# Linear attention with a top-2 mixture of experts on one core: early rows for four experts, the order of loads on two DMA queues, and longer gaps between row scatters

## The chip, the core and the metric

The kernel runs on one core of a Trainium2 chip. The core has a matrix engine (PE, with a separate record for its weight loads, PEld), a vector engine (DVE), a scalar engine (ACT), GpSimd (POOL) and a sync engine (SP). POOL and SP issue most of the transfers; all transfers of the core share 16 DMA engines. The metric is the device time in microseconds (us) of one execution. A run's time differs from execution to execution, so the median of several is compared. The profile comes from one execution; its span runs from the first to the last instruction.

## What is computed

```python
def _attn_ref(q, k, v):                       # q, k, v: 8 batches x 8 heads x 576 x 64
    q_p, k_p = phi(q), phi(k)                 # phi(x) = x + 1 if x > 0 else exp(x)
    kv = einsum('bhsd,bhse->bhde', k_p, v)
    z = sum(k_p, axis=2)
    num = einsum('bhsd,bhde->bhse', q_p, kv)
    den = einsum('bhsd,bhd->bhs', q_p, z)[..., None] + 1e-06
    return num / den

def _moe_ref(x, w_gate, w_noise, noise, w1, w2):    # x: 4608 tokens x 512
    noisy_logits = x @ w_gate + log1p(exp(x @ w_noise)) * noise     # 4608 x 8
    top2 = the two largest of each row; top2_w = their softmax
    for e in range(8):
        for k in range(2):
            mask = top2[:, k] == e
            h = maximum(x[mask] @ w1[e], 0.0)       # 512 -> 1024
            out[mask] += top2_w[mask, k, None] * (h @ w2[e])        # 1024 -> 512
```

Each token is thus worked on by two of eight experts. All matrix work is in bf16 with sums in float32.

## The kernel before

**Attention.** The tokens are taken in four groups of two batches (1152 tokens, nine columns of 128 each). For each group POOL issues the loads of k, q and v, in halves (L158, with a cast from float32 to bf16 on the way). ACT computes the exponential, DVE the rest of phi, PE the products; `num` (L262 to L295) makes x and the router's inputs: PE multiplies (L272), DVE divides (`rden` L279, `xr` L283, `lwt` L290).

**Routing.** `UNITS` cuts the tokens into five units: one for each of the first three groups, and two of six and three columns for the last. For each unit `rt_a`, `rt_b` and `rt_c` (L298 to L385) find the two experts of every token, its two gates and, with prefix sums on PE, its place `posi` in each expert's list. Each expert has two lists: "F" holds tokens for which it is the expert visited first (of lower number), "S" those which it visits second. `dispatch(u, a, z)` (L391) then writes the rows of x into these lists in device memory (`x_sorted`): for every column of 128 tokens and each of its two slots one indirect transfer issued by POOL (L398), followed by `apart()` (L387), a memset of a scratch tile `gap` on POOL that does nothing but take time. There are 72 such scatters.

**Early rows.** A list is complete only when all five units are dispatched. `ROUNDS` and `EARLY` (L34, L35) set bounds: after unit 0, 1 and 2, the places of the first `EARLY` experts' lists below a bound are known to be filled, because later ranks of those lists start at the bound at least (L380 to L384: the running count `carry` is raised to it). Blocks of early rows may be loaded before the later units are dispatched. Before the change the early blocks are of experts 0, 1 and 2: two blocks of expert 0 of two tiles each (a tile is 128 rows; the second of these is called `a1` in `attention` and `a0` in `routing`), then `a1` = (1, F, tiles 0 to 2), `b0` = (0, F, 4 and 5), `b1` = (1, F, 3 and 4), `a2` = (2, F, 0 to 3): 15 tiles, 1920 rows. The first block from complete lists is `c0` = (0, F, from tile 6).

**The experts.** `PLAN` lists the further blocks of every expert, of tiles of three kinds: F (first visits, result stored into `part`, L661 on SP), S (second visits: the first expert's result is gathered from `part` by L613 on POOL, added, and the sum scattered to the output by L667 on POOL), and M, a mixed tile with the ends of both lists, whose rows are gathered by `mid_gather` into `xm` (L499 to L509, POOL). `interval(cur, prev, weights, nxt)` (L677) writes down the order: `mm1` of the current block (L630 on PE, relu on ACT L632) alternates with `mm2` and `put` of the block before (L645 on PE; gate on DVE L649 to L653; store), and with the transposes of the next (L592 on PE, copy on ACT L596); then come the gathers of the next block and one or two halves of a later expert's weights (`w_load`, L438, issued by POOL at L442; 1 MB each as it lands). The table `todo` (L989 to L993) says with which block which half goes. Loads of rows (`xn_load`, L556 to L569) and of their gates (`meta_load`, L444 to L455) are issued by SP.

**What sets the order.** Attention and experts are written down in one fixed order per engine; nothing is rearranged. Each engine, and each issuing queue (POOL, SP), works through its instructions in that order, and an instruction that waits holds up all behind it. `general()` at the end is a fallback for lists that don't fit; it does no work on these inputs.

**Places that matter here.** The zero stores (in `attention`, L771 to L778) write `zrow`, a tile of zeros, over the rows that lie behind some lists' ends and are read as padding. Before, they stand on SP ahead of everything but a few loads. The weights of expert 0 are issued by POOL among the last columns of unit 0, those of expert 1 among `dispatch(1)`, those of expert 2 among `dispatch(3)`, those of expert 3 with the first two blocks of the main loop, and those of expert e+2 with the first two blocks of expert e.

Of the kernel before, what the change touches and what calls it, by code (L numbers as in the profile page):

```python
# [9 lines left out]
INT32 = mybir.dt.int32  # L10
# [23 lines left out]
ROUNDS = [(0, (256, 0, 0)), (1, (512, 384, 0)), (2, (768, 640, 512))]  # L34
EARLY = 3  # L35
# [14 lines left out]
def build_constants(tc, consts, w_gate, w_noise, noise):  # L50
# [23 lines left out]
    c["gap2"] = tile_("gap2", [P, 352])  # L74
    c["gap"] = c["gap2"][:, 0:192]
# [336 lines left out]
class PhaseB:  # L412


    def __init__(self, ctx, tc, w1, w2, x_sorted, part, out):
        self.tc, self.nc = tc, tc.nc
        self.w1, self.w2, self.x_sorted, self.part, self.out = w1, w2, x_sorted, part, out
        pool = lambda name, bufs: ctx.enter_context(tc.tile_pool(name=name, bufs=bufs, side="left"))
        self.wp = [pool("B_w", 2)]
        self.mp, self.xp, self.hp = pool("B_m", 2), pool("B_x", 3), pool("B_h", 2)  # L420
        self.yp = [pool("B_y", 3)]
        self.lp = self.np = None
        self.ps_h = self.ps_y = self.ps_t = None
        self.count = {}
        self.w, self.m, self.x = {}, {}, {}

        self.left, self.ready = [0] * 6 + [1] * 5 + [2] * 4, set()
# [329 lines left out]

def attention(pa, pb, c, x_sorted, zrow):
# [12 lines left out]
    nc.vector.memset(zrow[:], 0.0)  # L771

    for e, kind, i, n in ((0, "F", 8, 2 * P), (3, "F", 4, P), (4, "S", 4, P), (7, "S", 8, 2 * P), (E, "S", 0, 1)):
        row = pb.row(e, kind, i)
        for a in range(0, n, P):
            nc.sync.dma_start(out=x_sorted[row + a : row + min(n, a + P), :], in_=zrow[0 : min(P, n - a)])
    nc.sync.dma_start(out=pb.part[NO_P : NO_P + 1].bitcast(INT32)[:, 0 : ROW_W // 2], in_=zrow[0:1])
    nc.sync.dma_start(out=pb.part[NO_P : NO_P + 1].bitcast(INT32)[:, HD - ROW_W // 2 : HD], in_=zrow[0:1])  # L778
# [25 lines left out]
    for g in range(3):  # L804
# [4 lines left out]
        pa.phi(n, "k")  # L809
        if g < 2:  # L810
            pa.load(g + 2, "q")
# [71 lines left out]
def routing(pa, pb, c, first):  # L883
# [11 lines left out]
    pb.meta_load(2, "F", 0, 4, 2)  # L895
    pb.xn_load(a2, 2)
# [6 lines left out]
    pa.dispatch(3, 0, 3)  # L903
    pb.w_load(2, 0)
    pa.dispatch(3, 3, 6)
    pb.w_load(2, 1)
# [32 lines left out]
def kernel(  # L939
# [24 lines left out]
    with ExitStack() as order:  # L964
# [24 lines left out]
        todo = {0: (3, 0), 1: (3, 1)}  # L989
        for e in range(2, E - 2):  # L990
            at = [i for i, b in enumerate(blocks) if b["e"] == e][:2]
            for k, i in enumerate(at):
                todo[i] = (e + 2, k)  # L993
        for i, b in enumerate(blocks):
            pb.left += [b["e"]] * sum(kind != "S" for kind, _ in b["tiles"])
        for i, b in enumerate(blocks):
# [10 lines left out]
            if i in todo:  # L1007
                e2, k = todo[i]
                if k == 0 and e2 > 3:
                    pb.w_tiles(e2, {4: 1, 5: 2}.get(e2, 0))  # L1010
# [35 lines left out]
```

## Time and profile before

| | us |
|---|---|
| median of 7 runs | 462.21 |
| lowest, highest | 457.38, 466.95 |
| the profiled execution | 467.89 |
| its span | 466.0 |

| engine | busy us in the span | share |
|---|---|---|
| PE | 366.1 | 79% |
| PEld | 218.1 | 47% |
| DVE | 185.2 | 40% |
| ACT | 194.4 | 42% |
| POOL | 275.3 | 59% |

The mean granted clock of PE in that execution is 0.890 of full speed. The transfers move 85.59 MB at a mean of 184 GB/s.

How to read it: the shares are means over stages that differ. Attention lies in the first 160 us or so, with PE about half busy at most; the dispatches run on POOL from about 65 to 196; the experts' products fill PE behind that. Three views are used below. The windows give, for a stretch of time, the busy time of each engine with its number of instructions, the granted clock of PE and the mean busy share of the DMA engines (which can exceed one, since packets overlap). The chain of what ended last goes back from the last instruction: at every step to what released it. The timeline lists one engine's instructions with the idle time before each and what ended it. In them `x_sorted<-xr,posi` is a scatter of dispatch, `xn<-x_sorted` a load of rows, `xm<-x_sorted,m_idx` the gather of a mixed tile and `w<-in_moe_w_dram` a load of weights.

### The profile page before, as it was taken

The page shows a single profiled execution, that of the slowest core. Times are in us where ns is not written, and L with a number is a line of the kernel's source. Part 1 is how long each engine was busy: PE and PEld are TensorE (multiplying, and loading weights), DVE is VectorE, ACT ScalarE, POOL GpSimd, SP SyncE. Part 2 cuts the span into 40 slices and gives each one's busy share as a digit, 9 for nine tenths or more (in the row PEclk, how much of TensorE's full clock was granted, in tenths as well). Part 3 has the DMA queues.
Part 4 walks back from the last instruction along what each step waited for, and adds up shares of the span by engine and source line. Part 5 has one row for each costly group of instructions (what it writes and reads, how often), then busy time and mean ns, then how long its engine had stood idle before and what let it go on. Part 6 is the DMA issues. An engine that isn't in the chain of part 4 may idle for free.

```text
span 466.0 us, 7157 instructions
## 1 busy us (share of the span) xinstructions
PE 366.1 (79%) x2641; PEld 218.1 (47%) x2641; DVE 185.2 (40%) x471; ACT 194.4 (42%) x321; POOL 275.3 (59%) x408
## 2 busy tenths in 40 slices
PE   3594465663633688998999999799999899999990
PEld 1383454552511445543565545445555445554450
DVE  2737989895433564111233222041331131231231
ACT  1718562651520254543354553245345235445410
POOL 7120238988888158650036636349648865877781
PEclk9757767567975699999999999989999989999996
DMA  9999994797953339966349597985995996745531
GB/s 129 209 231 207 208 207 141 156 225 170 214 190 109 115 94 253 245 183 171 113 141 247 181 212 214 244 211 174 259 213 163 216 229 184 247 148 160 160 139 36
DMA packets 63010, 85.59 MB, mean 184 GB/s; under 512 B 15887, under 2 KB 45714, under 8 KB 62966
## 3 DMA queue, kind: packets, MB, share of 16 engines
q0 software_dynamic: 36160, 63.91, 61.9%
q1 hardware_dynamic: 25142, 20.96, 15.1%
q10 hardware_dynamic: 1664, 0.18, 0.5%
q8 instruction: 22, 0.36, 0.3%
q14 instruction: 22, 0.18, 0.1%
HBM read 83.88 MB, written 33.79 MB: 252 GB/s over the span
## 4 chain that ended last, share of the span: by engine, by line
PE 48%; DMA 23%; DVE 9%; POOL 8%; another core or an unknown queue 4%; issue 4%; ACT 2%; POOLq 0%; DVEq 0%; ACTq 0%; SPq 0%
PE b L630 23%; PE b L645 22%; DMA kq<-in_q_dram 5%; DMA xm<-x_sorted,m_idx 5%; POOL x_sorted L398 4%; DMA xn<-x_sorted 3%; PE t L592 3%; DMA w<-in_moe_w_dram 3%; DMA x_sorted<-xr,posi 3%; DMA kq<-in_k_dram 2%; DMA part<-y 1%; ACT e L178 1%; DVE xr L283 1%; POOL L L613 1%
## 5 line engine op out<-in xcount | busy, mean ns | idle before, releaser
L630 PE MATMUL b<-xt,w 128*128 128x256 bf16 (+5 forms) x832 | 152.7, 331 | 9.1 <-ACT xt L596 4.1
L645 PE MATMUL b<-w,hT 128*128 128x512 bf16 (+1 forms) x640 | 146.3, 384 | 0.0
L632 ACT ACTIVATE hT<-b 128x256 bf16<-128x256 f32 (+5 forms) x208 | 98.9, 484 | 104.1 <-PE b L630 95.3
L630 PEld LDWEIGHTS <-w 128*128 128x128 bf16 x832 | 81.2, 101 | 65.5 <-issue 13.1
L398 POOL DMA_INDIRECT x_sorted<-xr,posi x72 | 74.8, 1039 | 36.0 <-issue 25.2
L645 PEld LDWEIGHTS <-hT 128*128 128x128 bf16 (+1 forms) x640 | 59.6, 100 | 66.0 <-issue 5.6
L596 ACT COPY xt<-t 128x1024 bf16<-128x1024 bf16 x30 | 30.4, 1012 | 52.6 <-PE t L592 48.6
L613 POOL DMA_INDIRECT L<-part,mgi x12 | 12.0, 1001 | 56.8 <-DMA xn<-x_sorted 35.7
L178 ACT ACTIVATE e<-kq 128x2304 bf16<-128x2304 bf16 x16 | 33.3, 2123 | 25.3 <-DMA kq<-in_k_dram 9.5
L667 POOL DMA_INDIRECT out_dram<-y,si x34 | 33.8, 993 | 13.6 <-DVE y L649 8.8
L613 POOL DMA_INDIRECT L<-part,gi x34 | 34.8, 1023 | 6.9 <-issue 5.4
L272 PE MATMUL num<-kvbd,pqt 128*64 128x162 bf16 x288 | 17.6, 287 | 22.9 <-DVE lwt L290 20.6
L209 PEld LDWEIGHTS <-e 64*128 64x128 bf16 x288 | 21.8, 125 | 18.3 <-DVE e L190 13.8
L209 PE MATMUL b<-v,e 64*128 64x192 bf16 x144 | 20.4, 318 | 9.6 <-DVE e L190 6.5
L272 PEld LDWEIGHTS <-pqt 128*64 128x64 bf16 x288 | 14.4, 139 | 25.7 <-issue 14.6
L209 PE MATMUL misc<-v,e 64*128 64x192 bf16 x144 | 20.3, 318 | 5.8 <-DMA v<-in_v_dram 5.8
L592 PE MATMUL t<-ident,xn 128*128 128x128 bf16 (+1 forms) x256 | 20.5, 218 | 4.5 <-DMA xn<-x_sorted 3.4
L667 POOL DMA_INDIRECT out_dram<-y,msi x12 | 11.8, 979 | 20.8 <-DVE y L649 9.1
L592 PEld LDWEIGHTS <-xn 128*128 128x128 bf16 (+1 forms) x256 | 17.0, 98 | 13.1 <-DMA xn<-x_sorted 4.4
L651 DVE TENSOR_SCALAR y<-b,meta2F 128x512 f32<-128x512 f32 x14 | 10.4, 750 | 31.5 <-PE b L645 17.9
L283 DVE TENSOR_TENSOR xr<-num,rden 128x768 bf16<-128x768 f32 x24 | 21.9, 953 | 2.5 <-DMA x_sorted<-xr,posi 2.1
L389 POOL MEMSET gap<- 128x192 f32 x72 | 22.1, 306 | 0.0
(170 smaller groups left out, 362.8 us busy)
## 6 DMA issues: line engine op xcount, KB each, us to landing
w<-in_moe_w_dram POOLq DMA_DIRECT2D x16, 1024.0 KB
part<-y SPq DMA_DIRECT2D x39, 256.0 KB
kq<-in_k_dram POOLq DMA_DIRECT2D x8, 576.0 KB
kq<-in_q_dram POOLq DMA_DIRECT2D x8, 576.0 KB
v<-in_v_dram POOLq DMA_DIRECT2D x8, 576.0 KB
xn<-x_sorted SPq DMA_DIRECT2D x11, 256.0 KB
xn<-x_sorted SPq DMA_DIRECT2D x6, 384.0 KB
xn<-x_sorted SPq DMA_DIRECT2D x4, 512.0 KB
```

Of the source, the lines that this page charges most:

```text
L178: self.nc.scalar.activation(out=e, in_=x, func=ACT.Exp)
L209: nc.tensor.matmul(out=self.kvps[g, h, j][:, KVM * i : KVM * i + KVM], lhsT=e[half, hp, ci, :], rhs=v[half, hp::4, 64 * ci : 64 * ci + 64] ...
L272: nc.tensor.matmul(out=ps[half, hp, KVW * i : KVW * i + KVW], lhsT=self.pqt[g, 3 * t + i][:, hp, half], rhs=self.kvbd[g][:, j, hp, :], sta ...
L283: nc.vector.tensor_tensor(out=_ap(xr, [[64, 4], [ROW_W, 3], [1, 64]], off=3 * t * ROW_W + 256 * s), in0=_ap(ps, [[512, 4], [KVW, 3], [1, 6 ...
L398: r = self.nc.gpsimd.indirect_dma_start(out=self.x_sorted, out_offset=bass.IndirectOffsetOnAxis(ap=self.r["posi", u][:, ci - c0, sl : sl + ...
L592: nc.tensor.transpose(ps[:, i, dc, 0:m], self.xn(b, t, dc), self.c["ident"][0:m, 0:m])
L596: nc.scalar.copy(out=b["xt"][:, :, t * P : t * P + 2 * P].rearrange("p c (i r) -> p i c r", i=2), in_=ps)
L613: r = nc.gpsimd.indirect_dma_start(out=L[0:m].bitcast(INT32), out_offset=None, in_=self.part.bitcast(INT32), in_offset=bass.IndirectOffset ...
L630: nc.tensor.matmul(out=ps[:, 0:n], lhsT=w1[:, dc, fc * P : fc * P + P], rhs=b["xt"][:, dc, 0:n], start=(dc == 0), stop=(dc == 3))
L632: nc.scalar.activation(out=b["hT"][:, fc, 0:n], in_=ps[:, 0:n], func=ACT.Relu)
L645: nc.tensor.matmul(out=ps[i * m : i * m + m], lhsT=b["hT"][:, f, t * P : t * P + m], rhs=w2[:, f, :], start=(fc == 0), stop=(fc == 8 // n ...
L667: r = nc.gpsimd.indirect_dma_start(out=self.out, out_offset=bass.IndirectOffsetOnAxis(ap=self.m[e, kind, i]["si"][0:m], axis=0), in_=y[0:m ...
```

## The change

It has seven parts.

1. Early rows for a fourth expert: the bounds get a fourth column. The block of four tiles of expert 2 becomes two of two tiles (`a2`, `b2`), and a block `a3` of the first three tiles of expert 3 comes early: 18 tiles, 2304 rows in all. `a2` lies below the bounds of unit 1 and is taken right behind `a1`. Expert 3's plan loses the same three tiles.
2. The memset between dispatch scatters covers 288 elements for each partition, not 192; that after gathers and output scatters 416, not 352.
3. The zero stores move behind the first group's `phi(1, "k")` and stand in a function of their own.
4. Weights move on POOL's queue: expert 1's from `dispatch(1)` into the first columns of `dispatch(2)`; expert 2's from `dispatch(3)` into the last columns of `dispatch(2)`; expert 3's from the main loop into `dispatch(4)`. The weights of experts 4 to 7 are loaded one expert earlier, with the first two blocks of expert e-3.
5. The early rows' gates get tiles of their own, and the loads of all early blocks stand on SP ahead of the stores of the blocks they overlap: `a1` and `a2`, then `b0` and `b1` ahead of the first stores in `routing`, `b2` and `a3` ahead of those of the intervals.
6. The load of `c0` follows the fourth of the five early intervals.
7. The last early interval has no next block; the transposes of `c0` follow it.

```diff
-ROUNDS = [(0, (256, 0, 0)), (1, (512, 384, 0)), (2, (768, 640, 512))]
-EARLY = 3
+ROUNDS = [(0, (256, 0, 0, 0)), (1, (512, 384, 256, 0)), (2, (768, 640, 512, 384))]
+EARLY = 4
...
-    c["gap2"] = tile_("gap2", [P, 352])
-    c["gap"] = c["gap2"][:, 0:192]
+    c["gap2"] = tile_("gap2", [P, 416])
+    c["gap"] = c["gap2"][:, 0:288]
...
-        m = self.mp.tile([P, nt, 4], INT32, name=f"meta{nt}{kind}")
+        m = self.mp.tile([P, nt, 4], INT32, name=f"meta{nt}{kind}" if group is None else f"early{e}_{i0}")
...
+def zeros(pb, x_sorted, zrow):
+    nc = pb.nc
+    nc.vector.memset(zrow[:], 0.0)
+
+    for e, kind, i, n in ((0, "F", 8, 2 * P), (3, "F", 4, P), (4, "S", 4, P), (7, "S", 8, 2 * P), (E, "S", 0, 1)):
+        row = pb.row(e, kind, i)
+        for a in range(0, n, P):
+            nc.sync.dma_start(out=x_sorted[row + a : row + min(n, a + P), :], in_=zrow[0 : min(P, n - a)])
...
 def attention(pa, pb, c, x_sorted, zrow):
...
-    nc.vector.memset(zrow[:], 0.0)
-
-    for e, kind, i, n in ((0, "F", 8, 2 * P), (3, "F", 4, P), (4, "S", 4, P), (7, "S", 8, 2 * P), (E, "S", 0, 1)):
...
         pa.phi(n, "k")
+        if g == 0:
+            zeros(pb, x_sorted, zrow)
         if g < 2:
             pa.load(g + 2, "q")
...
         elif g == 1:
-            for i in range(2):
-                pa.dispatch(1, 3 * i, 3 * i + 3)
-                pb.w_load(1, i)
-            pa.dispatch(1, 6, 9)
+            pa.dispatch(1)
             pb.xn_load(a1, 1)
...
         else:
-            pa.dispatch(2)
+            for i in range(2):
+                pb.w_load(1, i)
+                pa.dispatch(2, i, i + 1)
+            pa.dispatch(2, 2, 5)
         pa.num(n, 0, 0)
...
-    a2, c0 = pb.block(2, ("F", 0, 4)), pb.block(0, ("F", 6, 4))
+    a2, b2 = pb.block(2, ("F", 0, 2)), pb.block(2, ("F", 2, 2))
+    a3, c0 = pb.block(3, ("F", 0, 3)), pb.block(0, ("F", 6, 4))
     pb.w_tiles(2, 1)
+    pb.w_load(2, 0)
+    pa.dispatch(2, 5, 7)
+    pb.w_load(2, 1)
+    pa.dispatch(2, 7, 9)
     pb.w_tiles(3, 1)
     pb.xn_load(a1, 1)
+    pb.meta_load(2, "F", 0, 2, 1)
+    pb.xn_load(a2, 1)
...
-    pa.dispatch(3, 0, 3)
-    pb.w_load(2, 0)
-    pa.dispatch(3, 3, 6)
-    pb.w_load(2, 1)
+    pa.dispatch(3)
...
-    pa.dispatch(4)
+    pa.dispatch(4, 0, 1)
+    pb.w_load(3, 0)
+    pa.dispatch(4, 1, 2)
+    pb.w_load(3, 1)
+    pa.dispatch(4, 2, 3)
     pb.mids()
-    pb.xn_t(b0, 0)
-    pb.interval(b0, a1, (), b1)
+    pb.xn_t(a2, 0)
+    pb.meta_load(2, "F", 2, 2, 2)
+    pb.xn_load(b2, 2)
+    pb.meta_load(3, "F", 0, 3, 2)
+    pb.xn_load(a3, 2)
+    pb.interval(a2, a1, (), b0)
+    pb.interval(b0, a2, (), b1)
+    pb.interval(b1, b0, (), b2)
+    pb.interval(b2, b1, (), a3)
     pb.prepare(0)
     pb.xn_load(c0)
-    pb.interval(b1, b0, (), a2)
-    pb.interval(a2, b1, (), c0)
-    return a2, c0
+    pb.interval(a3, b2, (), None)
+    pb.xn_t(c0, 0)
+    pb.xn_t(c0, 1)
+    return a3, c0
...
-    3: [[("F", 0, 4)], [("F", 4, 1), ("M", 0, 1), ("S", 0, 1), ("M", 1, 1)], [("S", 1, 2)]],
+    3: [[("F", 3, 2)], [("M", 0, 1), ("S", 0, 1), ("M", 1, 1)], [("S", 1, 2)]],
...
-        todo = {0: (3, 0), 1: (3, 1)}
-        for e in range(2, E - 2):
-            at = [i for i, b in enumerate(blocks) if b["e"] == e][:2]
+        todo = {}
+        for e in range(4, E):
+            at = [i for i, b in enumerate(blocks) if b["e"] == e - 3][:2]
             for k, i in enumerate(at):
-                todo[i] = (e + 2, k)
+                todo[i] = (e, k)
```

More of the change, by code (lines that the diff above doesn't have):

```diff
@@ L425, in __init__ @@
         self.w, self.m, self.x = {}, {}, {}
-        self.left, self.ready = [0] * 6 + [1] * 5 + [2] * 4, set()
+        self.left, self.ready = [0] * 6 + [1] * 5 + [2] * 4 + [3] * 3, set()
     def rot(self, pools, what):
@@ L755, in general @@
                             in_=b["y", 0][:], in_offset=None, bounds_check=N_TOK - 1, oob_is_err=False)
+def zeros(pb, x_sorted, zrow):
[5 more added lines that the diff above has]
+            nc.sync.dma_start(out=x_sorted[row + a : row + min(n, a + P), :], in_=zrow[0 : min(P, n - a)])
+    nc.sync.dma_start(out=pb.part[NO_P : NO_P + 1].bitcast(INT32)[:, 0 : ROW_W // 2], in_=zrow[0:1])
+    nc.sync.dma_start(out=pb.part[NO_P : NO_P + 1].bitcast(INT32)[:, HD - ROW_W // 2 : HD], in_=zrow[0:1])
 def attention(pa, pb, c, x_sorted, zrow):
@@ L770, in attention @@
     nc.vector.tensor_copy(out=wblk[64:P, :, 16:32], in_=wst[64:P])
-    nc.vector.memset(zrow[:], 0.0)
-    for e, kind, i, n in ((0, "F", 8, 2 * P), (3, "F", 4, P), (4, "S", 4, P), (7, "S", 8, 2 * P), (E, "S", 0, 1)):
[L774 to L778, printed above, removed]
     pa.rest()
@@ L894, in routing @@
     pb.xn_load(b1, 2)
-    pb.meta_load(2, "F", 0, 4, 2)
-    pb.xn_load(a2, 2)
     pb.xn_t(a1, 0)
@@ L1008 @@
                 e2, k = todo[i]
-                if k == 0 and e2 > 3:
+                if k == 0:
                     pb.w_tiles(e2, {4: 1, 5: 2}.get(e2, 0))
```

## The prediction

> **What bounds the kernel now.** I read the busy shares by window first, then the chain that ended last, then the PE and POOL timelines around each break of PE.
>
> The windows (length, then busy time and instructions of PE, PEld, DVE, ACT, POOL, then granted TensorE clock, DMA share, GB/s):
>
> ```profile
> 40.00:60.00 20.00, 9.71 (x147) 8.15 (x148) 18.50 (x36) 12.78 (x11) 4.07 (x6) 0.73 1.21 208
> 80.00:100.00 20.00, 10.30 (x126) 8.93 (x128) 17.61 (x52) 14.42 (x15) 18.06 (x24) 0.67 0.87 175
> 120.00:140.00 20.00, 8.92 (x118) 5.77 (x115) 7.94 (x33) 6.12 (x11) 17.46 (x29) 0.86 0.79 189
> 140.00:160.00 20.00, 7.86 (x53) 4.82 (x54) 9.02 (x24) 2.27 (x5) 12.46 (x20) 0.59 0.27 96
> 200.00:220.00 20.00, 16.59 (x97) 8.18 (x96) 3.27 (x12) 9.23 (x16) 6.55 (x9) 1.00 0.78 205
> 220.00:240.00 20.00, 20.00 (x129) 11.26 (x127) 6.91 (x16) 7.28 (x17) 0.24 (x1) 1.00 0.35 106
> 300.00:320.00 20.00, 18.19 (x99) 9.03 (x100) 5.60 (x12) 9.22 (x16) 10.57 (x15) 0.91 0.80 205
> ```
>
> Three stages. Attention (to about 106 us) is held by loads and by DVE. From 106 to about 158 nothing is full: PE works 8 to 9 of 20 us, DVE too, and POOL scatters rows. From 158 on PE is the bound: 20.00 of 20.00 in most windows, so there only PE's breaks can be won or added. The chain (start, length, what) and PE's timeline (last bracket: idle time before it and what ended it) name them:
>
> ```profile
> 108.36 3.38 DMA xt<-x_sorted
> 133.15 4.40 another core or an unknown queue
> 138.32 6.37 another core or an unknown queue
> 148.90 5.76 another core or an unknown queue
> 187.63 7.98 DMA x_sorted<-xr,posi
> 206.14 11.30 DMA xn<-x_sorted
> 289.06 12.71 DMA xm<-x_sorted,m_idx
> 364.14 9.76 DMA xm<-x_sorted,m_idx
> ```
>
> ```profile
> 195.91 1.89 PE L630 MATMUL b<-xt,w 128*128 128x512 bf16 x8 [0.90 <-DMA x_sorted<-xr,posi]
> 204.13 0.62 PE L592 MATMUL t<-ident,xn 128*128 128x128 bf16 x8 [1.16 <-DMA xn<-x_sorted]
> 217.49 0.62 PE L592 MATMUL t<-ident,xn 128*128 128x128 bf16 x8 [2.25 <-DMA xn<-x_sorted]
> ```
>
> So the wait for the complete lists costs PE 0.90+1.16+2.25 = 4.3 us. The gathered mixed tiles (xm) of experts 4 and 6 cost it 2.83 (298.98 to 301.81) and 2.55 (371.39 to 373.94). Between 127 and 155, 19.6 us of the chain (4%) belong to "another core or an unknown queue": finished PE matmuls whose results DVE and ACT see 3 to 6 us late.
>
> The sum is against the profiled execution: span 466.0, 1.9 outside it, 467.9, which is 5.7 over the median 462.2. I add the difference to the median.
>
> **The change, part by part.**
>
> Longer gaps. 192 elements take 0.275 us, 352 take 0.413 (both in POOL's timeline): 0.86 ns an element, so 288 take 0.358 and 416 take 0.469. The 72 dispatch gaps add 72 x 0.083 = 6.0 us to POOL; the some 100 gaps of the second half add 5.5. The latter are hidden: POOL works 12 of 20 us there and stood 32 us at 208 to 240. The first 12 precede the last q load on POOL, so that load, both weight loads of expert 0 and the first rows slip by 1.0. That chain is on the path: +1.0.
>
> Zero stores. 0.87 MB leave the start and come back at about 45 us. In the start, halves of k (0.59 MB) land every 2.84 us and with the stores between them every 4.1 to 4.4, so the stores cost the loads 2.8 us. But ACT waited 1.6 for q, and DVE only 0.28 (it was busy until 47.9). Gain: 0.3 and the zrow memset's 0.3 on DVE. The Trainium skill, "DMA: Bandwidth & Descriptors", section "Issuing engines are not separate DMA queues", speaks against more: all initiated DMAs share the same 16 engines and interleave. The row of 40 to 60 says the same (DMA share 1.21, full until about 72): moved bytes are paid there, unless DVE covers them (18.50 of 20). Full price 2.8, full gain 2.8; I take -0.4. Section sum: +0.6. The rule bears equally on the row loads put ahead of the stores on SP: they wait less for their turn (before: up to 9 us behind y), but the bytes travel with the same weights. I count nothing for it alone.
>
> Weights of experts 1 to 3 on POOL. An issue takes 0.95 + 0.2, six of them move, none is added. Expert 1's pair leaves dispatch(1), which with longer gaps still ends at about 129 (before 128.5). Then, at 1.49 a scatter: w(1,0) to 130.4, one column, w(1,1) to 134.5, columns to 146.4. Its first use is at 168.67 (the first matmuls on 384 columns); the slowest weight load of the chain took 12.8, so both halves land by 148. w(2,0) now stands in dispatch(2) and needs the space of attention's last tiles, so it waits for the last num matmul on PE. That one ended at 149.6 but was seen at about 154.7, with the front's slip 155.7. Behind it: four columns (12 us), w(2,1), then 12 scatters of dispatch(3), and dispatch(4) with w(3): 170, 188, 200. Before they ended at 153.95, 184.8, 195.9: the 13.45 us that POOL stood idle before 167.40 are used up. Rows of group 2 land at about 175, b0's load takes 3.4, PE wants it at 182.7: covered. w(2,0) is wanted where b0 had its first matmuls, 177.51, and issued 21 us before: covered. w(3) is wanted at 209 and issued by 199: just covered; 5 us later it would be PE's stall.
>
> More early rows. The block of four tiles of expert 2 is cut in two and three tiles of expert 3 come early: 64 matmuls more, but half as wide (8 of 256 columns 0.87 us, 8 of 512 1.73), so PE's time changes by nothing. 16 more relus of 0.48 on ACT lie in a stage where ACT works 9 of 20. The three tiles are 3 x (1.75 + 1.73) = 10.4 us of PE ahead of the first block from a complete list, which PE then wants at 217.7. Its rows: last scatter 200, landing 4 later as before (195.9 to 199.9), up to 5 more behind w(3,1), and a load of 3.7 (quick) to 11.3 (the slow one of the chain): 208 to 220. Taken: all of the 4.3 us goes; ends 0 and -5.5.
>
> Later weights, one expert earlier. Expert 7's pair no longer travels when expert 6's xm is gathered: -2.55, and the clock. Here the row and a rule differ. After each xm stall eight 256-wide matmuls took 1.71 instead of 0.87 and the windows show 0.91: about 1.3 us. The rule ("TensorE: Matmul & The Clock Gate", Part 1: the clock is halved after an idle window of about 3.4 us) would make that 0 for stalls of 2.8 and 2.55. The trace decides: -3.9; by the rule alone it would be -2.55.
>
> Expert 4's xm loses cover: the block before it has no F tile, and the one before that two for four. So two mm2 tiles (3.46) and some mm1 (1.7 to 2.3) leave between issue and use: wanted 16 us after the interval's start instead of 22, landed at 24.7 as before behind a weight load. The stall grows from 2.8 to at most 8.7; two 256 KB stores fewer should hasten it. Ends 0 and +5.9, taken +4.5. Expert 3's xm now goes behind two weight loads instead of one; DVE waits 5 to 7 us longer there, PE has four banks of work: 0, at worst +3.
>
> Own buffers for early metas remove a 9 us wait on SP, off the path. Three wider bounds: under 0.5 us of DVE in idle time.
>
> Sum: +0.6 - 4.3 - 3.9 + 4.5 = -3.1: 459.1 against 462.2.
>
> **The rivals.**
>
> B, front shrinks. The late results between 127 and 155 coincide with 18 scatters 1.41 apart; the last came when that burst ended (153.95). If the burst causes it, spacing of 1.49 and a pause at w(2,0) cut the 19.6 us; everything behind, up to posi(3) at 166, moves. At half: -10, so 449. For it: the coincidence. Against: no record names the cause, and dispatch(1) made the same scatters without such waits.
>
> C, slower: POOL stands before w(2,0) for PE's last num. With the old lateness there are 9 us or less of slack for the complete lists (208 to 220 against 217.7). Expert 1's weights, 2 MB in all, now fall into the same 130 to 150 us as dispatch(2), where the DMA share was only 0.27 in the window from 140. If that makes the last num later by 8 to 12, then columns 5 to 8, dispatch(3), w(3) and c0's rows all slip as much: 8 to 12 less some cover, on top of -3: 467 to 472. It decides once that wait ends after about 163. For it: the queue order and a chain that is already PE, DVE, ACT in turn there. Against: POOL's pause also lightens the DMA.
>
> D: early rows don't move PE, since the wait shifts onto c0 whole and xm takes back the rest: 462.
>
> **How the numbers follow.** A, the sum above, 0.42 (459; own range 454 to 464), B 0.25 (447 to 453), C 0.28 (466 to 473), D 0.05. Runs of this kernel scatter by about 1%, so 1% is what can be told: faster is below 457.6, slower above 466.8. A gives faster 0.17, same 0.24, slower 0.01; B faster 0.25; C slower 0.28; D same 0.05. Range: 447 to 471 leaves out the ends of B and C.
>
> **What would show it.** In the new profile: PE without a break over 1 us between 180 and 220 (early rows), or one on DMA xn at about 217 (C, D). The idle time before w(2,0) on POOL, and when dispatch(3) starts: 170 in A, 162 or less in B, 178 or more in C. The share of "another core or an unknown queue": 4% in A, 2% in B. PE idle on xm at expert 6 gone, at expert 4 from 2.8 to 7 us. Zero stores showing up as a longer wait of DVE or of the first scatters before 72 us would make the front's term wrong; a PE stall on w anywhere would make the weight terms wrong.

## The result and the profile after

| | kernel before | changed kernel |
|---|---|---|
| median, us | 461.26 (63 runs) | 458.08 (26 runs) |
| lowest, highest | 454.67, 467.73 | 454.27, 461.33 |
| span of the profiled execution | 466.0 | 455.7 |

The ratio of the two is 0.9978, with a 95% interval of 0.9955 to 1.0: no change beyond 0.5%. It is nearer to one than the medians, because the comparison leaves out the runs that lie more than 1.5% above the quickest of their kernel, and 28 of the 63 runs of the kernel before do. The forecast was 459.1 and a gain of 3.1; by the ratio the gain is about 1, a third of that.

Four windows of the changed kernel (busy times of PE, PEld, DVE, ACT, POOL, then PE's clock, DMA share, GB/s), the end shares of its chain, and PE's breaks from its timeline:

```profile
120.00:140.00 20.00, 13.65 (x155) 10.11 (x153) 14.56 (x51) 7.98 (x16) 17.73 (x27) 0.83 0.62 142
140.00:160.00 20.00, 14.60 (x90) 8.62 (x89) 9.35 (x40) 5.88 (x13) 16.73 (x26) 0.83 1.15 269
200.00:220.00 20.00, 17.73 (x113) 10.06 (x111) 3.20 (x12) 10.41 (x21) 5.92 (x8) 1.00 0.47 135
280.00:300.00 20.00, 13.73 (x96) 8.66 (x93) 3.73 (x13) 7.29 (x15) 13.29 (x18) 0.84 1.07 261
```

```profile
PE 58%; POOL 14%; DMA 13%; DVE 6%; issue 4%; ACT 2%; SPq 0%; POOLq 0%; DVEq 0%; ACTq 0%
```

```profile
150.53 1.01 PE L592 MATMUL t<-ident,xn 128*128 128x128 bf16 x8 [3.46 <-DMA xn<-x_sorted]
...
212.27 0.60 PE L592 MATMUL t<-ident,xn 128*128 128x128 bf16 x8 [1.10 <-ACT xt L596]
213.83 1.67 PE L630 MATMUL b<-xt,w 128*128 128x448 bf16 x8 [0.95 <-ACT xt L598]
...
296.44 0.61 PE L592 MATMUL t<-ident,xm 128*128 128x128 bf16 x4 [6.26 <-DMA xm<-x_sorted,m_idx]
```

What to see: "another core or an unknown queue", 4% of the chain before, is gone, and PE and DVE do in 120 to 160 about 1.7 and 1.4 times what they did there before. The complete lists no longer stop PE, but in their place it waits 1.10 and 0.95 for the copies of the first complete block's transposes. Expert 4's gathered tile stops it for 6.26 instead of 2.83, expert 6's not at all. And there is a wait that was not forecast: 3.46 us for the rows of the second block (1, F, 0 to 2), at 150.53.

Unit 3's first scatter comes at 161.68 on POOL, where the prediction's own sum (A) had 170 and its rival B 162 or less (the changed kernel's scatters of that unit follow without a pause). B had also forecast a smaller share without a releaser than A.

The profile of the kernel before, which the prediction was read from, and this one differ by 10 us of span, the medians by 3. The first question is therefore whether the late results are part of the kernel before at all.

### The profile page after: what moved, and what is told of

The parts are those of the page before. It is cut to its first block, busy times and chain, and to the rows that moved or that the text cites. A ratio compares the mean times of both kernels' runs of the same rounds, so it can differ in the third digit from the quotient of the medians.

```text
span 455.7 us, 7309 instructions
## 1 busy us (share of the span) xinstructions
PE 365.9 (80%) x2705; PEld 225.5 (49%) x2705; DVE 185.3 (41%) x474; ACT 196.2 (43%) x337; POOL 285.5 (63%) x408
## 4 chain that ended last, share of the span: by engine, by line
PE 58%; POOL 14%; DMA 13%; DVE 6%; issue 4%; ACT 2%; SPq 0%; POOLq 0%; DVEq 0%; ACTq 0%
PE b L645 25%; PE b L630 24%; POOL x_sorted L398 5%; DMA v<-in_v_dram 4%; PE t L592 3%; POOL out_dram L667 3%; DMA x_sorted<-xr,posi 2%; POOL L L613 2%; DMA x_sorted<-zrow 2%; DMA xm<-x_sorted,m_idx 2%; DMA xn<-x_sorted 2%; POOL gap L389 2%; ACT xt L596 2%; PE num L272 1%; PE misc L209 1%
## 5 line engine op out<-in xcount | busy, mean ns | idle before, releaser
L632 ACT ACTIVATE hT<-b 128x256 bf16<-128x256 f32 (+5 forms) x224 | 100.4, 461 | 100.6 <-PE b L630 91.9
L630 PEld LDWEIGHTS <-w 128*128 128x128 bf16 x896 | 86.5, 99 | 59.8 <-issue 13.5
L651 DVE TENSOR_SCALAR y<-b,early 128x512 f32<-128x512 f32 x18 | 13.5, 750 | 44.5 <-PE b L645 38.6
L272 PE MATMUL num<-kvbd,pqt 128*64 128x162 bf16 x288 | 17.8, 293 | 11.5 <-DVE lwt L290 10.1
L389 POOL MEMSET gap<- 128x288 f32 x72 | 26.8, 372 | 0.0
L190 DVE TENSOR_TENSOR e<-e,kq 128x2304 bf16<-128x2304 bf16 x16 | 21.4, 1355 | 0.3
```

The lines of the kernel that those rows point to most:

```text
L272: nc.tensor.matmul(out=ps[half, hp, KVW * i : KVW * i + KVW], lhsT=self.pqt[g, 3 * t + i][:, hp, half], rhs=self.kvbd[g][:, j, hp, :], sta ...
L389: self.nc.gpsimd.memset(self.c["gap"], 0.0)
L630: nc.tensor.matmul(out=ps[:, 0:n], lhsT=w1[:, dc, fc * P : fc * P + P], rhs=b["xt"][:, dc, 0:n], start=(dc == 0), stop=(dc == 3))
L632: nc.scalar.activation(out=b["hT"][:, fc, 0:n], in_=ps[:, 0:n], func=ACT.Relu)
```

## The experiments

The kernels were run in groups, each on one chip and beside the kernel before; numbers of two groups are compared only where the kernel before is at the same level in both, and then with care. The kernel before came out at two levels, and all its runs of a group lay at the same one: about 447 in three groups, about 463 in two; the result, with 461, was taken at the upper one. The first group (447) and the third (464) ran on the same chip, so the level does not belong to the chip. What sets it no record tells.

| group | kernel before | kernel | median | ratio to before, 95% |
|---|---|---|---|---|
| 1 | 447.2 | the kernel before again | 447.9 | 1.0016 (0.9988 to 1.0044) |
| 1 | | before, long gaps | 453.8 | 1.0133 (1.0083 to 1.0183) |
| 1 | | changed, old gaps | 452.3 | 1.0113 (1.0066 to 1.016) |
| 1 | | changed, transposes inside | 453.8 | 1.0144 (1.0095 to 1.0194) |
| 2 | 463.0 | the changed kernel | 460.8 | 0.9945 (0.9913 to 0.9977) |
| 2 | | changed, expert 1's weights at the old place | 458.7 | 0.9898 (0.985 to 0.9947) |
| 2 | | changed, weights of 6 and 7 a block later | 455.2 | 0.9818 (0.9776 to 0.9861) |
| 2 | | four edits together, old gaps | 469.0 | 1.0113 (1.0071 to 1.0155) |
| 3 | 463.8 | before, long gaps | 454.4 | 0.9822 (0.9752 to 0.9891) |
| 3 | | changed, old gaps | 463.3 | 1.0041 (1.0011 to 1.0071) |
| 3 | | two repairs | 450.8 | 0.9756 (0.9703 to 0.9809) |
| 3 | | two repairs, gaps from unit 2 on | 447.8 | 0.9656 (0.959 to 0.9722) |
| 4 | 446.3 | the changed kernel | 455.5 | 1.0218 (1.0168 to 1.0268) |
| 4 | | before, gaps from unit 2 on | 450.2 | 1.008 (1.0037 to 1.0122) |
| 4 | | changed, weights 4 to 7 at the old place | 454.5 | 1.0197 (1.0145 to 1.025) |
| 4 | | changed, zero stores early | 456.0 | 1.0222 (1.0172 to 1.0272) |
| 5 | 447.5 | two repairs, old gaps | 442.5 | 0.9878 (0.9832 to 0.9925) |
| 5 | | two repairs, gaps from unit 2 on | 443.0 | 0.9893 (0.9855 to 0.9931) |

"Two repairs" stands for the edits to the weights of experts 6 and 7 and to the transposes, shown below. The changed kernel is thus slower by 2.2% at one level of the kernel before and quicker by 0.6% at the other.

**The kernel before again, and the gaps alone.** The first kernel has no edit. The second:

```diff
-    c["gap2"] = tile_("gap2", [P, 352])
-    c["gap"] = c["gap2"][:, 0:192]
+    c["gap2"] = tile_("gap2", [P, 416])
+    c["gap"] = c["gap2"][:, 0:288]
```

> The kernel before, once more, for a profile of an execution near its median. Theory 1 (the late PE results between 127 and 155 us are an accident of single executions, and the change's own effect lies in the part bound by PE): the first matmuls on 384 columns start at 158 to 161, as in the changed kernel (158.56), 'another core or an unknown queue' is under 1% of the chain, the span is 455 to 460, and PE's breaks at 196 to 218 and at the gathered tiles of experts 4 and 6 are there again, 4.3, 2.8 and 2.6 within 1 each. Theory 2 (the lateness belongs to the old order of scatters and weight loads and the change took it away): the first 384-column matmul is at 163 or later, and 3% or more of the chain is again without a releaser.

> The kernel before with the longer memsets alone (288 and 416 elements). Theory 1: 0 to +1.0 us (twelve gaps more of 0.083 ahead of the last q load; the rest under cover), spread of the executions as before. Theory 2, if the gaps are what cures the late results: -2 to -4 on the median, and the spread falls from about 13 us to about 7.

The kernel before again, windows and then POOL's timeline over the place where the prediction had found POOL idle, down to the last scatter (the memset between two scatters is left out):

```profile
120.00:140.00 20.00, 13.62 (x146) 8.77 (x144) 15.84 (x53) 6.92 (x13) 17.69 (x29) 0.83 0.79 195
140.00:160.00 20.00, 14.71 (x108) 9.03 (x106) 12.03 (x79) 9.63 (x25) 17.69 (x29) 0.93 0.52 157
```

```profile
149.37 1.00 POOL L398 DMA_INDIRECT x_sorted<-xr,posi  x1 [0.16 <-issue]
150.81 0.97 POOL L398 DMA_INDIRECT x_sorted<-xr,posi  x1 [0.16 <-DVE noisy L322]
152.21 0.97 POOL L398 DMA_INDIRECT x_sorted<-xr,posi  x1 [0.17 <-ACT hT L632]
...
179.42 0.97 POOL L398 DMA_INDIRECT x_sorted<-xr,posi  x1 [0.16 <-issue]
```

Span 442.2, nothing of the chain without a releaser. Without late results `posi` of unit 3 is ready in time, and POOL goes from unit 2's last scatter (150.81, the 54th of 72) to unit 3's first (152.21) without a pause, where the first profile has 13.45 us of idle time. From 80 to 160 POOL is as good as full, 17.7 to 17.8 of every 20 us. The first 384-column products start at 148.02, ten us ahead of theory 1 and fifteen ahead of theory 2. So the long gaps have no cover: their 72 x 0.083 = 6.0 show whole, last scatter 185.51 instead of 179.42, and +6 in time. Theory 1 was right that the lateness is not always there, and wrong that the gaps then cost at most 1.0. It was also wrong about PE's breaks: 1.93 and 1.48 before rows of complete lists, none at expert 4's gathered tile and 1.60 at expert 6's.

**The old gaps in the changed kernel, and the transposes.** The first is the edit above the other way round; the second:

```diff
-    pb.interval(a3, b2, (), None)
-    pb.xn_t(c0, 0)
-    pb.xn_t(c0, 1)
+    pb.interval(a3, b2, (), c0)
```

> The changed kernel with the old memsets (192 and 352 elements). Theory 1: 0 to -1.0 us against the changed kernel, so 457 to 458. Theory 2, if the gaps cure the late results: +2 to +4, unexplained waits back in the chain, executions up to 467.

> The changed kernel with the transposes of the first complete-list block back inside the last early interval. In the changed kernel they stand behind it, and PE waits 1.10 and 0.95 for the copies at 211 to 214. If that exposure is what took back part of the 4.3 us: -1.0 to -2.0 against the changed kernel. If the complete lists are not there any earlier: 0 to +1, with PE waiting on the load of rows at about 205 instead.

The old gaps gave 1.0113 where the changed kernel has 1.0218 (group 4): they are worth about 1% where results are not late, and theory 2 falls for this level. The transposes inside gave 1.0144; the intervals overlap with the changed kernel's, so no gain is shown by time. The trace shows the two breaks gone and 1.46 us for the load of the first complete block's rows, at 207.09, in their place.

**Group 2: the changed kernel, two of its parts, and a mixture.**

The first two edits are expert 1's weights at the old place, and the weights of experts 6 and 7 a block later; the mixture has both, with the transposes inside and the old gaps.

```diff
         elif g == 1:
-            pa.dispatch(1)
+            for i in range(2):
+                pa.dispatch(1, 3 * i, 3 * i + 3)
+                pb.w_load(1, i)
+            pa.dispatch(1, 6, 9)
...
-            for i in range(2):
-                pb.w_load(1, i)
-                pa.dispatch(2, i, i + 1)
-            pa.dispatch(2, 2, 5)
+            pa.dispatch(2, 0, 5)
```

```diff
-            at = [i for i, b in enumerate(blocks) if b["e"] == e - 3][:2]
+            at = [i for i, b in enumerate(blocks) if b["e"] == e - 3][(e > 5):][:2]
```

> The changed kernel once more, beside the kernel before. Theory P (where PE's results are not late, POOL is the bound of the front: in the undisturbed profile of the kernel before it scatters without a break from 64 to 180 us, so 72 longer gaps cost 6 us there and no cover is left): where the kernel before takes about 447, this takes 453 to 456, 1.3 to 2% slower, last scatter at 189 to 191. Theory E (the two are equal whatever the execution): within 0.5% of the kernel before in the same call.

> The changed kernel with expert 1's two weight halves back among dispatch(1). In the changed kernel they load beside the second block's rows and PE waits 3.5 to 4.8 us for those rows at 147 to 151, with a slow clock behind. If the loads cause it: that wait is under 1 us, the first matmuls on 384 columns start 5 to 7 us earlier (151 to 154), but the end moves by less, 0 to -3, since the last scatter on POOL stays at about 190 and the complete lists become the wait again (a PE break of 2 to 6 us on x_sorted or xn at 195 to 210). If the rows are slow for another reason: nothing moves at 147 to 151.

> The changed kernel with the weights of experts 6 and 7 issued one block later, so that the mixed tile of expert 4 is gathered ahead of the first of them. If the weight load is what makes that gather land late: PE's break of 5.5 to 6.3 us at 290 to 297 and the slow clock behind it (2.7) go, -6 to -8.5 us, with at most 1 us coming back at experts 5 and 6. If the block is simply too short for the gather: the break shrinks by no more than 2.

> The changed kernel with four things together: old memsets (192, 352), expert 1's weights back in dispatch(1), the transposes of the first complete-list block inside the last early interval, and the weights of experts 6 and 7 one block later. Theory P: the front as in the kernel before (last scatter near 182), the early rows' cover without its price: 440 to 444 where the kernel before takes 447, -1 to -1.5%. If early rows bring nothing even then: 446 to 449.

The weights of experts 6 and 7 a block later gave -5.6 against the changed kernel of the group, a little less than the 6 to 8.5 expected. From PE's timeline of that kernel:

```profile
296.19 0.40 PE L592 MATMUL t<-ident,xm 128*128 128x128 bf16 x4 [0.67 <-DMA xm<-x_sorted,m_idx]
```

The break at expert 4 was 6.71 in the changed kernel of this group and is 0.67: it was the weight load ahead of the gather in POOL's queue (in the changed kernel of group 4 it is issued at 283.45 and the gather at 284.61; here no weight load stands there). Expert 1's weights at the old place took the wait for the second block's rows away, as expected: their load is issued at 145.51 and the transposes start at 150.25 without a wait. But PE's results came late in that run (a break of 7.58 before the last `num`, which also moved everything behind it), the first 384-column products came at 155.79, not at 151 to 154, and the 2 us of time are within the intervals. No new break came at the complete lists.

The mixture was forecast at 440 to 444 beside a kernel before of 447. Beside one of 463 it came out at 469, the worst of all. From the chain of that kernel, in order of time:

```profile
127.83 5.33 another core or an unknown queue
134.62 0.95 DVE xr L283
136.09 7.29 another core or an unknown queue
...
153.05 10.40 DMA xn<-x_sorted
...
179.01 3.64 another core or an unknown queue
183.16 2.41 another core or an unknown queue
185.62 2.91 another core or an unknown queue
```

The late results are back, at the stretches where POOL scatters with the old gaps. Theory P knew nothing of them. The load of the second block's rows takes 10.40 us here and stops PE for 6.07, though expert 1's weights have their old place: beside it travels the first half of expert 2's, issued at 149.50. So expert 1's weights are not the only thing that can stretch this load. The new theory, G: at the level of 463 PE's results are seen late while POOL scatters every 1.41 us, and scatters every 1.49 us take most of that away; at the other level there is no lateness, and the gaps only cost. Its rival, W: the order of the weight loads cures it.

**Group 3: the gaps alone again, both ways, and the repairs.** The first two kernels are those of group 1. The third has the two edits for the weights of experts 6 and 7 and for the transposes, called the two repairs below; the fourth also:

```diff
-    def apart(self):
+    def apart(self, u):
-        self.nc.gpsimd.memset(self.c["gap"], 0.0)
+        self.nc.gpsimd.memset(self.c["gap"] if u >= 2 else self.c["gap2"][:, 0:192], 0.0)
```

> The longer memsets alone once more, since the kernel before takes about 447 on one chip and about 462 on another. Theory G (where the kernel before takes about 462, the 15 us more are PE results seen late while POOL scatters every 1.41 us, and scatters every 1.49 us take most of that lateness away; where it takes 447 there is none, and the gaps only cost their 6 us): beside a kernel before of about 462: 453 to 457, -1 to -2%, under 1% of the chain without a releaser; beside one of about 447: 453 to 455 as measured already. Theory W (the order of weights cures it, not the gaps): beside 462: 463 to 469.

> The changed kernel with the old memsets once more. Theory G: beside a kernel before of about 462: 463 to 470 with 3% or more of the chain without a releaser, so that the whole gain of the changed kernel comes from the gaps; beside one of about 447: 452 to 453 as measured already. Theory W: beside 462: 457 to 460.

> The changed kernel with the weights of experts 6 and 7 one block later and the transposes of the first complete-list block back inside the last early interval, long memsets kept. The two act at different places, so they should add: beside a kernel before of 462, 453 to 455 (the first alone gave 455.2 there); beside 447, 445 to 448 (454 less 6 to 8.5).

> The same, with the long memset only from the third unit's scatters on (the first 36 scatters have the old one): POOL's chain is 3 us shorter. Theory G with the lateness belonging to the stretch of the third and fourth unit alone: -1 to -3 against the run beside it on any chip. If short gaps earlier already bring the lateness back: +3 or more where the kernel before takes 462.

The kernel before was at 464 here, on the chip of the first group. The shares of the chain by engine, first of the kernel before with long gaps, then of the changed kernel with old ones:

```profile
PE 55%; DMA 18%; POOL 8%; DVE 7%; issue 6%; ACT 3%; another core or an unknown queue 1%; POOLq 0%; ACTq 0%; DVEq 0%; SPq 0%
```

```profile
PE 66%; DVE 8%; DMA 7%; issue 6%; ACT 6%; POOL 3%; another core or an unknown queue 2%; POOLq 0%; DVEq 0%; ACTq 0%
```

G holds by time on both sides: the very edit that costs 6 us in group 1 brings 9.4 here by the medians, 1.8% by the ratio, and the changed kernel without it is where the kernel before is. W falls. The edit also lengthens the memset of the second half, which no run separates. By the share without a releaser the case is weaker than forecast: 1% and 2%, not under 1% and over 3%. The 2% are one piece of 8.02 us at 72.22, where ACT waits for PE; PE's last product there ended at 78.0 and ACT went on at 80.26, so some 2 us of it are lateness. The rest of the lateness shows under another name: PE stands for 8.60 us before 171.32, put down to a scatter, but its transposes had ended at 162.7 and ACT began to copy them only at 170.26. Under long gaps some is left too: a break of 7.82 before the last `num` in the first kernel.

The two repairs brought 0.9756 (450.8, below the 453 to 455 expected), the gaps from unit 2 on 0.9656. The second was meant to be 1 to 3 below the first and is 3.0 below; the intervals touch. By time, then, long gaps for the last 36 scatters do as well. But the lateness does not belong to these alone: in the second kernel, where the first 36 have the old gap, PE's product of 78.2 reaches ACT at 80.57, as it does late in the profile before (78.2 and 80.54); in the kernel before with long gaps of this group ACT goes on at 77.81.

**Group 4: the parts, at the level of 446.** The kernel before with the gaps from unit 2 on has the edits of the gaps and of `apart`. The others are the weights of experts 4 to 7 at the old place, and the zero stores early:

```diff
-            at = [i for i, b in enumerate(blocks) if b["e"] == e - 3][:2]
+            at = [i for i, b in enumerate(blocks) if b["e"] == e - 2][:2]
```

```diff
-        if g == 0:
-            zeros(pb, x_sorted, zrow)
...
+    zeros(pb, x_sorted, zrow)
     pa.rest()
```

> The changed kernel again, as the reference of this call. Beside a kernel before of about 447: 453 to 456 (theory P: the price of the gaps, the gathered tile of expert 4 and the late rows of the second block, without anything to cure). Beside one of about 462: 458 to 461, as measured already.

> The kernel before with the long memsets only from the third unit's scatters on. If the late results belong to the stretch of those units alone: beside 462, 450 to 453, 2 to 4 below the same kernel with all gaps long (454.4). If the earlier short gaps bring them: 458 or more. Beside 447: 450 to 451 (36 gaps of 0.083 = 3 us).

> The changed kernel with the weights of experts 4 to 7 at their old place, two experts ahead instead of three. The prediction's two terms: PE's wait for the gathered tile of expert 6 comes back (2.5 and 1.3 of slow clock, +3.9), while expert 4's tile keeps its break of 5.5 to 6.3, since it stays behind one weight load either way: +3 to +4.5 in all against the changed kernel of this call. If expert 4's break shrinks too, the earlier weights are what made it grow: -4 to 0.

> The changed kernel with the zero stores back at the start. The prediction's term: +0.3 to +0.6 (they delay the first loads by 2.8 us, of which DVE hides all but 0.3, and their memset costs DVE 0.3). If the middle of the attention is what pays for them: -0.5 to -2.5, and the wait of the first scatters at 64 to 84 is shorter.

The changed kernel came out at 455.5, where 453 to 456 was expected for this level. Half of the gaps cost 3.9, where 3 was expected, within the error. The zero stores make no difference that can be told. The old place of the weights was to cost 3 to 4.5 and gave 1.0 less, within the intervals: the earlier weights bring nothing here. PE's timeline of that kernel:

```profile
291.41 0.61 PE L592 MATMUL t<-ident,xm 128*128 128x128 bf16 x4 [4.97 <-DMA xm<-x_sorted,m_idx]
...
361.91 0.40 PE L592 MATMUL t<-ident,xm 128*128 128x128 bf16 x4 [1.36 <-DMA xm<-x_sorted,m_idx]
362.14 1.04 PE L630 MATMUL b<-xt,w 128*128 128x256 bf16 x8
```

Expert 6's break is back, but with 1.36 and no slow clock behind it (eight matmuls in 1.04, not 1.91), and expert 4's is a little shorter.

The changed kernel of this group is the one to hold against the kernel before of group 1, both without late results. From its PE timeline, and from SP's and the chain, the reason of its first break:

```profile
149.47 1.01 PE L592 MATMUL t<-ident,xn 128*128 128x128 bf16 x8 [4.77 <-DMA xn<-x_sorted]
...
294.36 0.61 PE L592 MATMUL t<-ident,xm 128*128 128x128 bf16 x4 [5.63 <-DMA xm<-x_sorted,m_idx]
```

```profile
131.41 8.69 SPq L661 DMA_DIRECT2D part<-y  x2
140.20 0.46 SPq L566 DMA_DIRECT2D xn<-x_sorted  x1
```

```profile
140.20 9.14 DMA xn<-x_sorted
```

The rows of the second block still stand behind two stores on SP. Their load is issued at 140.20 (138.29 before) but takes 9.14 us, in a window (140 to 160) with a DMA share of 1.07 where the kernel before has 0.52. Expert 1's weights, issued at 128.23 and 132.11, now travel about there, then expert 2's (147.69), and the rows of `a2` directly behind.

The spans differ by 11.2 (453.4 and 442.2; by the medians 9.2). PE's windows up to and from the first products of the first complete block, first of the kernel before again, then of this one:

```profile
0.00:195.91 195.91, 130.00 (x1221) 91.55 (x1222) 120.88 (x344) 90.46 (x126) 125.39 (x200) 0.80 0.93 198
195.91:430.00 234.09, 231.01 (x1419) 123.63 (x1419) 61.64 (x125) 103.62 (x195) 145.91 (x205) 1.00 0.75 198
```

```profile
0.00:210.62 210.62, 139.91 (x1306) 101.09 (x1315) 124.75 (x351) 95.64 (x142) 132.89 (x201) 0.81 0.93 200
210.62:442.00 231.38, 222.30 (x1368) 122.24 (x1391) 59.68 (x122) 100.59 (x195) 150.02 (x204) 0.99 0.70 186
```

PE is idle for 65.9 and 70.7 up to that block, +4.8, and for 3.1 and 9.1 behind it, +6.0. This trace lacks 32 of 2705 matmuls, so its idle time reads somewhat too long; the complete traces of the changed kernel (the result's, and group 1's with old gaps) both have PE busy for 365.9, against 361.4 here before. By these, an estimate, some 4.5 of the 11.2 are longer busy time, mostly the slow clock behind the breaks, and 6.7 idle time. In the first part the first 384-column products are 9.1 late (157.10 and 148.02), more than half of it the wait for the second block's rows; from there to the first complete block PE is idle for 5.5 instead of 6.7, so little of it is won back. In the second part the two breaks at expert 4 are 1.58 (rows) and 5.63 (gathered tile), where the kernel before has 1.48 within the first complete block and 1.60 at expert 6.

**Group 5: can both be had.**

> The changed kernel with the weights of experts 6 and 7 one block later, the transposes of the first complete-list block inside the last early interval, and the old memsets everywhere. Beside a kernel before of about 447: 442 to 446 (changed kernel with old memsets 452.3 there, less 6 to 8.5 for the gathered tile and up to 2 for the transposes). Beside one of about 462: 455 to 461 (old memsets 463.3 there, less the same), slower than the run beside it.

> The same with the long memset from the third unit on, once more. Beside a kernel before of about 447: 445 to 448, within 0.5% of the kernel before (3 us of gaps against what the two repairs bring). Beside one of about 462: 447 to 450, as measured already (-3.4%).

Two repairs with the old gaps: 442.5 beside 447.5. With the gaps from unit 2 on: 443.0, where 445 to 448 was expected: the 36 long gaps, 3 us on POOL, cost 0.5 here, within the intervals. The latter's PE timeline keeps the break at the second block's rows and two small ones at the first complete block and at expert 4:

```profile
146.79 0.60 PE L592 MATMUL t<-ident,xn 128*128 128x128 bf16 x8 [3.08 <-DMA xn<-x_sorted]
...
202.46 0.62 PE L592 MATMUL t<-ident,xn 128*128 128x128 bf16 x8 [0.15 <-DMA xn<-x_sorted]
...
283.92 0.40 PE L592 MATMUL t<-ident,xm 128*128 128x128 bf16 x4 [1.49 <-DMA xm<-x_sorted,m_idx]
```

This kernel, the changed one with two repairs and the long gap from unit 2 on, beats the kernel before at both levels: 0.9893 (0.9855 to 0.9931) and 0.9656 (0.959 to 0.9722). What is left of the change is worth having once the two things that the repairs take off are gone; the early rows by themselves were not run.

## Why the prediction was off

The sum was a gain of 0.7%, the measured one 0.2%. That the sign is right and the total near is luck: terms of opposite sign that the sum did not hold nearly cancel. At the level at which the result was taken, the long gaps alone brought about 8 to 9 us (forecast: a loss of 1), and the rest of the change, run without them, nothing or a loss of up to 2 (forecast: a gain of 4.1). The two do not add up to the 2 us of both together (group 2); why is open.

**The step that failed** is the cost of the longer gaps. "The 72 dispatch gaps add 72 x 0.083 = 6.0 us to POOL" was right to the tenth. What failed is the cover: only the first twelve were charged, +1.0, because in the profiled execution POOL stood idle for 13.45 us before 167.40. "From 106 to about 158 nothing is full" overlooked POOL in the prediction's own rows, 17.46 of 20 from 120 to 140. The idle time came from the late results themselves, which held up `posi` of unit 3. Without them POOL has hardly any idle time from 80 us to the last scatter (the longest pause behind unit 2 is 1.68), and the gaps cost 6; with them the gaps cure more than they cost, -9.4. Neither is +1.0. The same profile named the lateness (19.6 us, "another core or an unknown queue"), and rival B had this very mechanism: scatters 1.41 apart delay what PE has finished, and 1.49 helps, with -10. It was given 0.25, on the ground that dispatch(1) made the same scatters without such waits. It was near in size for the gaps alone, and its signs came nearest (unit 3's scatters at 161.68; no share without a releaser, where B had 2% and A 4%); what it missed is what the rest of the change costs.

**Early rows.** The 4.3 us were 3.4: the break of 0.90 at 195.91 stands before products of expert 2's early block (512 columns), and ACT's copy of their transposes ended at 195.86, so it was no wait for complete lists. In the profile after no break on a complete list is left. But a last interval without a next block leaves the transposes of the first complete block bare: 2.05 come back. The change's part 7 says so; the prediction put it at nothing. And with the transposes inside, a break of 1.46 on the load returns, so the cover was not quite long enough either.

**Expert 4's gathered tile.** Forecast +4.5, a break growing from 2.8 to at most 8.7; measured 5.5 to 6.7 with the slow clock behind it, where the weights come early. In the profile after, sixteen matmuls then took 4.61 instead of some 1.9: 6.26 and 2.7, against 2.83 and 1.3 before, +4.8. Right in size; group 2 shows that it is the weight load ahead of the gather that makes it. At the level of 447 it is more, since the kernel before has no break there (group 1).

**Expert 6's gathered tile.** Forecast -3.9; the break went, but its size in the kernel before varies: 2.55 in the first profile, 1.21 to 1.84 in three others (again, or with longer gaps) with no slow clock behind it, 3.08 with a slow clock in group 1's kernel with long gaps. At the level of 447 the term was 1.6, or 1.4 by the old place of the weights, and taking the weights back cost no time there.

**Expert 1's weights.** They were checked for their own date ("first use is at 168.67 ... land by 148") and did meet it. What stands beside them was not counted: the load of the second block's rows takes 9.14, and PE waits 3.1 to 4.8 us for it, with a slow clock behind. Rival C saw the 2 MB fall into this stretch, but for the last `num`, not for these rows. The prediction's own rule, that moved bytes are paid where they go, was applied to the zero stores and not here. That expert 1's weights are the cause is argued: their old place took the wait away in one run, and in the mixture the load was as long without them.

**w(2,0) and rival C.** It waited 0 us for attention's last `num`: dispatch(2)'s own scatters kept POOL until 147.60. C's wait and its price did not occur. The zero stores' -0.4 and the early metas' 0 are within what cannot be told.

**What would have shown it.** The prediction took an execution 5.7 us above the median as the pattern for the queue's idle time. Time that an engine stands idle behind an unexplained wait is not cover: it goes when the wait goes.

Left open: what makes PE's results late and what sets the level, which the same chip shows both ways; whether 36 long gaps are enough at the late level (by time one run of one kernel speaks for it, while the first unit's results came late there); why the gaps' gain and the rest do not add up at that level; and whether it is expert 1's weights, expert 2's or the rows of `a2` that delay the second block's rows (the first were moved back at the late level only, the others never).

## What to carry to other kernels

Before slack on a queue is used as cover, ask what made it: slack behind a wait that nothing in the profile explains is gone in the next execution. Take a second profile of the kernel before when the first lies above the median, and price a spacing instruction on a queue that feeds the critical path at its full sum, unless what waits for the end of that queue has cover of its own (6.0 for 72 gaps in the kernel before, 0.5 for 36 in the one with two repairs). When loads are moved, look for the transfers that stand beside them at the new place, not only for their own date; and a gather that stands behind a weight load needs as much cover as the weight load takes.

## What the hardware showed

- Scatters of 128 rows, issued every 1.41 us by POOL, went in some groups with results of PE that DVE and ACT saw late, and in others not, on the same chip: in the profile before, products that ended at 78.2 and 149.6 were seen at 80.54 and 154.68; in the changed kernel with old gaps of group 3, transposes that ended at 162.7 were seen at 170.26. A gap of 0.358 instead of 0.275 us between the scatters was worth 1.8% in the one case and cost 1.3% in the other. That the scatters cause the lateness is not shown beyond this.
- PE's slow clock after a break. At the gathered tiles the granted clock fell to 0.5 behind every break of 2.42 us and more (2.42, 2.55, 2.83, 3.08, and 4.97 to 6.71), and behind the twelve of 0.64 to 2.12 eight matmuls on 256 columns took 1.04, as at full clock. The first instructions do not tell: in the kernel before with long gaps (group 1) the transposes still ran at full speed, and the matmuls behind them did not:

```profile
289.90 0.40 PE L592 MATMUL t<-ident,xm 128*128 128x128 bf16 x4 [2.42 <-DMA xm<-x_sorted,m_idx]
290.14 1.79 PE L630 MATMUL b<-xt,w 128*128 128x256 bf16 x8
```

  The changed kernel of group 2 does the same behind a break of 3.10 at 150.32: the clock was 1.00 for 0.7 us, then 0.62 and 0.50. The Trainium skill ("TensorE: Matmul & The Clock Gate", Part 1) gives an idle window of about 3.4 us that runs freely; by that figure the breaks of 2.42 to 3.08 would have cost no clock, and these runs show that they did.
